# A fused chunk attention and SoLU feed-forward kernel: products with low words last in the first tiles, a new list of opening steps, six scalings and eight loads on GpSimd

## The chip, the cores and the metric

The kernel runs on one core of a Trainium2 chip. The metric is the device time of one launch in microseconds, of which the lower is the better; it is given as the median of several runs. A profiled execution is a run of its own, and its span (first to last instruction) is what the rows below are taken from.

The engines are named as the profile names them: PE (TensorE) with PEld for its weight loads, DVE (VectorE), ACT (ScalarE), POOL (GpSimd), and SP (SyncE), which here only issues DMAs. Each engine runs its instructions in the order of the program and waits where an instruction's data or buffer is not ready, so whatever stands behind a waiting instruction on its engine waits too.

## The reference

Attention inside chunks of 64 positions, and on its output (4608 tokens of 512 features) a feed-forward layer with a SoLU activation and a layer norm. Inputs are q, k and v of shape (8, 8, 576, 64) in float32; the weights w_in (512 x 1024), w_out (1024 x 512) and g_ln come in float64.

```python
scores = scale * np.matmul(q_c, k_c.transpose(0, 1, 2, 4, 3))   # chunks of 64
scores = scores - np.max(scores, axis=-1, keepdims=True)
attn = np.exp(scores)
attn = attn / (np.sum(attn, axis=-1, keepdims=True) + 1e-09)
out = np.matmul(attn, v_c)
...
h = x @ w_in
e = np.exp(h - np.max(h, axis=-1, keepdims=True))
solu = h * (e / (np.sum(e, axis=-1, keepdims=True) + 1e-09))
mu = np.mean(solu, axis=-1, keepdims=True)
var = np.mean((solu - mu) ** 2, axis=-1, keepdims=True)
ln = (solu - mu) / np.sqrt(var + 1e-06) * g_ln
return (ln @ w_out).astype(np.float32)
```

## The kernel before

**Tiles.** The 4608 tokens are 36 tiles of 128 (NT = 36). A tile passes through scores (16 small products of q and k), a softmax, values (16 small products of the attention weights and v), which give x, the first product h = x w_in (`ffn_in`, L469), the activation (`solu_a`, `solu_b`, `variance`), a transposition of z, and the second product (`ffn_out`, L587), whose result is scaled and stored.

**High and low words.** Products run on fp32r operands, so each of x, z and the weights is split in a high word and a low word (x_h and x_l, z_h and z_l, wi_h and wi_l, wo_h and wo_l), and three of the four products of words are summed: high with high, high with low, low with high. `ffn_in` is thus 24 products of 128x512 (4 chunks of the 512 features, 2 halves of the columns, 3 pairs of words), and `ffn_out` is 24 as well (8 chunks, 3 pairs). In `ffn_in` of tile 0 and in every `ffn_out`, the three pairs of a chunk come together, so a chunk's low words must be there when its high words are used.

**Weights.** The float64 weights arrive as 8 blocks of 1 MB (`load_pair`, L158, the tile w_raw), 4 of w_in and 4 of w_out. A block x is made into words by five steps: `unit_scale` (c:x, a clamp on POOL or DVE, then an activation on ACT), `unit_bits` (b:x), `unit_join` (C:x on DVE), `unit_high` (t:x on ACT) and `unit_low` (d:x on DVE). The buffers of blocks 2 to 7 are those that later hold q and k (q_st, k_st).

**The opening.** What happens before tile 5's first product is not a loop but a list of words, `START` (L18): a word names a step and a tile or block, and a word that comes a second or third time is the next part of that step. n loads q and k of one tile as they lie (nat), N transposes them on PE and copies them out of PSUM (qT, kT), v loads v, S is scores, A the maximum, the subtraction and the exponential of the softmax, B its sum, reciprocal and scaling (s_e or e), T a transposition of the attention weights on PE with four copies to attn_t, V values with x_h and x_l, M is `ffn_in`, X and Y are `solu_a` and `solu_b`, R is `variance`, z the transposition of z on PE with z_h and z_l, F a third of an `ffn_out`, o and O the scaling and the store of a tile's result, w some products of the identity matrix with no use but to keep PE at work. U and Z transpose on DVE (a_b, z_b) and, at every second tile, send 8 and 16 DMAs that finish the transposition (attn_t, z_t); half of them are issued by POOL, half by SP. Q and q load q and k of a whole batch (batch 2 here) in 32 DMAs of 32 partitions by 18 runs of 128 bytes (`qk_loads`, L253), 16 of q and 16 of k, all issued by SP; K turns them on DVE for tile 9.

`MOVED` (L34) lists the steps that run on another engine than their usual one: a copy out of PSUM on DVE in place of ACT, a clamp, `unit_bits` or the last step of `solu_b` on POOL.

**The order.** Every engine keeps the order in which the code calls it, so the list alone sets the order on each engine during the opening.

**The loop.** From tile 5 on a loop (L753) runs all tiles alike: `z_split` of the tile whose second product comes next, `ffn_in(i)`, at odd i the scores and values of the two tiles that follow, then the three thirds of an `ffn_out` of a tile three back, with the other engines' steps between. Tile 5's `ffn_in` is the loop's first work on PE; behind it stand scores of tile 8, values of tile 6, scores of 9 and values of 7, and then tile 2's `ffn_out`. `z_turn(4)` and one store are the first steps of the loop on DVE and SP.

Of the kernel before, what the change touches and what calls it, by code (L numbers as in the profile page):

```python
# [18 lines left out]
n:0 w:3 N:0:0 N:0:0 w:1 N:0:1 N:0:1 g w:1 S:0 A:0 G P:0 P:0 n:1 A:0 c:0 c:0 w:3 N:1:0 N:1:0 w:1  # L19
N:1:1 b:0 N:1:1 G P:1 w:1 S:1 B:0 v:0 C:0 A:1 t:0 T:0 T:0 c:1 c:1 w:4 V:0 V:0 P:2 b:1 c:2 n:2  # L20
d:0 P:3 A:1 n:3 w:6 N:2:0 w:1 N:2:1 C:1 V:0 B:1 t:1 c:2 T:1 N:2:0 b:2 N:2:1 T:1 d:1 S:2 n:4
M:0 M:0 C:2 t:2 c:3 c:3 v:1 A:2 A:2 b:3 d:2 C:3 N:3:0 N:3:1 N:3:1 M:0 N:3:0 S:3 N:4:0 B:2 N:4:1
t:3 N:4:0 A:3 P:5 d:3 c:5 N:4:1 A:3 T:2 T:2 S:4 V:1 M:0 P:4 n:5 B:3 T:3 V:1 V:1 M:1 X:0 X:0 T:3
A:4 A:4 b:4 v:2 N:5:1 c:4 n:6 P:7 c:5 N:5:0 c:4 Y:0 Y:0 n:7 N:5:1 V:2 b:5 v:3 B:4 N:5:0 V:2 b:7
C:4 z:0:1 P:6 v:5 N:6:0 X:1 v:4 C:5 N:6:0 S:5 Q:2 q:8 t:4 V:2 d:4 N:6:1 N:6:1 X:1 t:5 A:5 Y:1
M:2 z:0:1 z:0:1 X:2 A:5 R:0 z:0:0 z:0:0 q:8 N:7:1 q:8 c:6 S:6 Y:1 V:3 X:2 T:4 T:4 z:0:0 d:5 F
V:3 Y:2 Y:2 N:7:0 A:6 c:6 c:7 V:3 b:6 B:5 C:6 n:8 N:7:0 M:3 R:1 c:7 q:8 N:7:1 C:7 T:5 z:1:0 t:6
T:5 S:7 t:7 d:6 X:3 X:3 d:7 V:4 V:4 Y:3 Y:3 R:2 z:1:1 A:6 F F A:7 V:4 z:1:0 z:1:0 v:6 Z:2 A:7
M:4 F B:7 Z:3 o:0 V:5 z:1:1 z:1:1 B:6 F F v:7 O:0 X:4 N:8:0 X:4 U:6 U:7 V:5 Y:4 V:5 K:9 Y:4 N:8:0
R:4 R:3 N:8:1 N:8:1 o:1  # L30
# [32 lines left out]
def chunk_attention_then_solu_ffn(  # L63
# [523 lines left out]
    def ffn_out(i, part, parts):  # L587
# [8 lines left out]
        ops = []  # L596
        for fc in range(NFC):
            ops += [
                (zh[:, fc, :], wo_l[:, fc, :]),
                (zh[:, fc, :], wo_h[:, fc, :]),  # L600
                (zl[:, fc, :], wo_h[:, fc, :]),
            ]
# [251 lines left out]
```

## Time and profile before

| | us |
|---|---|
| median of 3 runs | 474.69 |
| lowest, highest | 474.67, 475.53 |
| the profiled execution, its own time | 479.38 |
| its span | 477.6 |
| its mean granted TensorE clock | 0.996 of full speed |

The profiled execution is 1.78 us longer than its span and 4.69 us longer than the median of the runs. In its page PE is busy for 98% of the span, DVE for 78%, ACT for 54%, POOL for 31%. A busy PE includes products whose ends are modelled, so the share says where PE had something in hand, and the waits are read from the time between the starts of instructions. The opening fills about the first 80 us, the loop the rest but for a tail of some 20 us.

### The profile page before, as it was taken

The numbers are of one execution on the slowest core, as the hardware profiler recorded it, in microseconds if no ns is written. First come the engines' busy times: TensorE is split into PE (matmuls) and PEld (weight loads), VectorE is DVE, ScalarE is ACT, GpSimd is POOL, SyncE is SP. The second block draws the span as 40 slices with busy tenths as digits, with TensorE's granted clock in tenths as the row PEclk, the third lists the DMA queues.
The fourth block names the chain that finished last, engine by engine and source line by source line (L and its number), as shares of the span: only waits on it lengthen the run. The fifth ranks groups of instructions, "written<-read, shape, count | busy, mean of one in ns | idle before, by whom it ended". The sixth has DMA issues, their size and how long they took to land.

```text
span 477.6 us, 11116 instructions
## 1 busy us (share of the span) xinstructions
PE 467.3 (98%) x4212; PEld 384.2 (80%) x4212; DVE 374.9 (78%) x520; ACT 256.5 (54%) x423; POOL 147.9 (31%) x298
## 2 busy tenths in 40 slices
PE   7899999899999999999999999999999999999997
PEld 5677778688888888888888888888888888888876
DVE  3999998787869887878788979797979797954441
ACT  2879884436445545454554545455555454545452
POOL 2212726050505050505050505132414142323330
PEclk9999999899999999999999999999999999999999
DMA  8999979768776878686348596848643535343221
GB/s 220 305 284 227 199 132 189 176 167 158 176 143 152 162 167 174 165 168 153 97 119 168 138 184 146 180 115 189 146 124 90 133 87 135 83 118 102 75 59 75
DMA packets 192924, 72.57 MB, mean 152 GB/s; under 512 B 177188, under 2 KB 177960, under 8 KB 191976
## 3 DMA queue, kind: packets, MB, share of 16 engines
q1 hardware_dynamic: 186056, 58.76, 55.6%
q0 software_dynamic: 6528, 12.86, 10.3%
q8 instruction: 33, 0.54, 0.5%
q10 hardware_dynamic: 288, 0.26, 0.2%
q14 instruction: 19, 0.16, 0.1%
HBM read 36.70 MB, written 9.44 MB: 97 GB/s over the span
## 4 chain that ended last, share of the span: by engine, by line
PE 86%; DVE 4%; DMA 4%; SPq 3%; ACT 2%; issue 1%; ACTq 0%; DVEq 0%
PE po L54 38%; PE ph L54 38%; PE tp L54 5%; PE sx L54 5%; SPq L54 3%; DMA nat<-in_q_dram 2%; DMA z_t<-z_b 1%; ACT attn_t L54 1%; ACT wo_h L54 1%; ACT z L54 1%; DVE z_b L54 1%; DVE h_nmax L54 0%; DMA attn_t<-a_b 0%; DVE s_sum L54 0%; DVE z L54 0%
## 5 line engine op out<-in xcount | busy, mean ns | idle before, releaser
L54 ACT ACTIVATE z<-ph,h_nmax 128x1024 f32<-128x1024 f32 x36 | 40.2, 1117 | 140.3 <-DVE h_nmax L54 140.3
L54 PE MATMUL po<-wo_l,z_h 128*128 128x512 f32 (+1 forms) x288 | 113.3, 393 | 0.1
L54 PE MATMUL ph<-wi_l,x_h 128*128 128x512 f32 x288 | 112.9, 392 | 0.0
L54 PE MATMUL ph<-wi_h,x_h 128*128 128x512 f32 x288 | 112.2, 390 | 0.0
L54 PE MATMUL po<-wo_h,z_l 128*128 128x512 f32 (+1 forms) x288 | 111.8, 388 | 0.0
L54 PE MATMUL po<-wo_h,z_h 128*128 128x512 f32 (+1 forms) x288 | 111.3, 386 | 0.0
L54 POOL DMA_DIRECT2D z_t<-z_b x144 | 71.8, 506 | 28.8 <-DVE z_b L54 24.6
L54 PE MATMUL ph<-wi_h,x_l 128*128 128x512 f32 x288 | 78.3, 390 | 0.0
L54 POOL TENSOR_TENSOR u<-ssq,eps 128x1 f32<-128x1 f32 x36 | 7.1, 198 | 214.7 <-ACT sq L54 214.4
L54 DVE TENSOR_REDUCE h_nmax<-ph 128x1 f32<-128x1024 f32 x36 | 44.0, 1222 | 31.3 <-PE ph L54 31.3
L54 PEld LDWEIGHTS po<-wo_l,z_h 128*128 128x128 f32 x288 | 54.1, 188 | 11.8 <-ACT z_h L54 0.5
L54 PEld LDWEIGHTS ph<-wi_l,x_h 128*128 128x128 f32 x288 | 54.1, 188 | 11.8 <-issue 0.4
L54 PEld LDWEIGHTS ph<-wi_h,x_l 128*128 128x128 f32 x288 | 53.9, 188 | 12.0 <-DVE x_l L54 0.7
L54 PEld LDWEIGHTS po<-wo_h,z_l 128*128 128x128 f32 x288 | 54.1, 188 | 11.7 <-DVE z_l L54 0.4
L54 PEld LDWEIGHTS ph<-wi_h,x_h 128*128 128x128 f32 x288 | 54.1, 188 | 11.0
L54 PEld LDWEIGHTS po<-wo_h,z_h 128*128 128x128 f32 x288 | 54.1, 188 | 10.5
L54 DVE TENSOR_TENSOR z_l<-z_t,z_h 128x1024 fp32r<-128x1024 f32 (+1 forms) x37 | 42.0, 1136 | 23.8 <-ACT z_h L54 22.5
L54 DVE SCALAR_TENSOR_TENSOR z<-ph,z 128x1024 f32<-128x1024 f32 x36 | 43.9, 1220 | 13.3 <-ACT z L54 13.2
L54 ACT ACTIVATE z<-z,z_sum 128x1024 f32<-128x1024 f32 x33 | 38.1, 1153 | 22.9 <-DVE z L54 22.4
L54 DVE STREAM_TRANSPOSE z_b<-z 128x1024 f32<-128x1024 f32 x34 | 41.2, 1211 | 6.2 <-ACT z L54 3.1
L54 ACT CAST z_h<-z_t 128x1024 fp32r<-128x1024 f32 (+1 forms) x37 | 35.9, 971 | 9.3 <-PE po L54 6.5
L54 ACT ACTIVATE o_sb<-po,r 128x512 f32<-128x512 f32 (+1 forms) x36 | 24.2, 673 | 27.3 <-POOL r L54 18.6
(76 smaller groups left out, 602.8 us busy)
## 6 DMA issues: line engine op xcount, KB each, us to landing
out_dram<-o_sb SPq DMA_DIRECT2D x35, 256.0 KB, 2.5
v_sb<-in_v_dram SPq DMA_DIRECT2D x32, 256.0 KB, 4.5
z_t<-z_b POOLq DMA_DIRECT2D x128, 64.0 KB, 2.7
z_t<-z_b SPq DMA_DIRECT2D x128, 64.0 KB, 2.9
q_st<-in_q_dram SPq DMA_DIRECT2D x96, 72.0 KB, 3.0
k_st<-in_k_dram SPq DMA_DIRECT2D x96, 72.0 KB, 3.2
w_raw<-in_moe_w_out_dram SPq DMA_DIRECT2D x4, 1024.0 KB, 7.9
attn_t<-a_b POOLq DMA_DIRECT2D x60, 64.0 KB, 3.8
```

The lines of the kernel that those rows point to most:

```text
L54: ins = make(*args, **kwargs)
```

## The change

It touches the opening list, four places in the code that the list calls, and one line of the loop.

- **Order of products.** `ffn_in` of tile 0 sums the pairs with wi_h for all four chunks first, in four parts (before: in parts of six with wi_l in them), and the pairs with wi_l last. `ffn_out` of tile 0 takes the pairs with wo_h first and those with wo_l last; of tiles 1 to 31 the pairs with z_h first and those with z_l in the last third; tiles 32 to 35 keep the old order. The number of products stays.
- **The list.** `START` is written anew. Block 1 of w_in is loaded whole and first, the tiles' q and k come in earlier places, and the eight first-part `ffn_out` words and both stores stand in the list (the loop's one store goes).
- **Engines.** The scaling of the softmax of tiles 0, 3, 4, 5, 6 and 7 and wi_l of block 3 move from DVE to POOL, `unit_bits` of block 0 to POOL and of block 7 to DVE, the clamp of block 1 to DVE. Of the copies out of PSUM eight run on DVE, before three. The last step of `solu_b` is on POOL for tiles 2 and 3 and on DVE for tile 4 (before: POOL for 0, 1 and 3).
- **Loads of k.** Of batch 2, the eight loads of k with heads 4 to 7 are issued by POOL.
- **Identity products.** 7 of 512 columns in place of 22 of 256.

```diff
 MOVED = """
-N:0:0=dve N:8:0=dve N:8:1=dve Y:0=pool Y:1=pool Y:3=pool b:7=pool c:0=pool c:1=pool c:2=pool
-c:3=pool c:4=pool c:5=pool c:6=pool c:7=pool
+B:0=pool B:3=pool B:4=pool B:5=pool B:6=pool B:7=pool N:0:0=dve N:0:1=dve N:1:0=dve N:1:1=dve
+N:2:0=dve N:4:0=dve N:5:0=dve N:8:0=dve Y:2=pool Y:3=pool Y:4=dve b:0=pool c:0=pool c:2=pool
+c:3=pool c:4=pool c:5=pool c:6=pool c:7=pool d:3=pool
...
-            sync.dma_start(
+            by_pool = b == 2 and src is k and h >= H // 2
+            (pool if by_pool else sync).dma_start(
...
-            sums.sort(key=lambda s: s[1])
+            sums = [(n, cc, m) for cc in range(NCC) for m in (1, 2) for n in range(2)]
+            sums += [(n, cc, 0) for cc in range(NCC) for n in range(2)]
...
-            if i == 0 and at and at % 6 == 0:
+            if i == 0 and at and at % 4 == 0:
...
+        h = NFC // 2
+        if i == 0:
+            ops = hh[:h] + lh[:h] + hh[h:] + lh[h:] + hl
+        elif i < NT - 4:
+            ops = [x for both in zip(hl, hh) for x in both] + lh
+        else:
+            ops = [x for each in zip(hl, hh, lh) for x in each]
...
-        m = ident.unsqueeze(1).to_broadcast([P, 2, P])
+        m = ident.unsqueeze(1).to_broadcast([P, 4, P])
...
             z_turn(i - 1)
-            store_one(i)
             load_batch(next_batch)
```

**SP near the end of the opening.** Before, from the loads of q of batch 2 to the attention DMAs of tiles 6 and 7 (q_st and k_st are the loads of batch 2, z_t the DMAs of tiles 2 and 3, attn_t those of tiles 6 and 7):

```order
L54 DMA q_st<-in_q_dram 32x18x32 x16
L54 DMA k_st<-in_k_dram 32x18x32 x8
L54 DMA nat<-in_q_dram 128x8x64
L54 DMA nat<-in_k_dram 128x8x64
L54 DMA k_st<-in_k_dram 32x18x32 x8
L54 DMA v_sb<-in_v_dram 128x8x64
L54 DMA z_t<-z_b 32x512 x8
L54 DMA v_sb<-in_v_dram 128x8x64
L54 DMA out_dram<-o_sb 128x512
L54 DMA attn_t<-a_b 32x512 x4
```

With the change the same stretch of SP is:

```order
L55 DMA q_st<-in_q_dram 32x18x32 x16
L55 DMA v_sb<-in_v_dram 128x8x64
L55 DMA k_st<-in_k_dram 32x18x32 x8
L55 DMA nat<-in_q_dram 128x8x64
L55 DMA nat<-in_k_dram 128x8x64
L55 DMA z_t<-z_b 32x512 x8
L55 DMA v_sb<-in_v_dram 128x8x64
L55 DMA attn_t<-a_b 32x512 x4
L55 DMA out_dram<-o_sb 128x512 x2
```

Eight loads of k and one store no longer stand ahead of the attention DMAs.

**POOL in the same part of the opening.** Before, from the small steps of `variance` of tile 1 (u and r) to the attention DMAs; the TENSOR_SCALAR on z is the last step of `solu_b` of tile 3:

```order
L54 TENSOR_TENSOR u<-ssq,eps 128x1
L54 TENSOR_TENSOR r<-u,mhalf 128x1
L54 TENSOR_SCALAR z<-z,z_sum 128x1024
L54 TENSOR_TENSOR u<-ssq,eps 128x1
L54 TENSOR_TENSOR r<-u,mhalf 128x1
L54 DMA z_t<-z_b 32x512 x8
L54 DMA attn_t<-a_b 32x512 x4
```

With the change, from the same u and r of tile 1; s_e is the scaling of tile 5, e_97 and e_98 those of tiles 6 and 7:

```order
L55 DMA k_st<-in_k_dram 32x18x32 x8
L55 TENSOR_TENSOR s_e<-e_98,s_rinv 128x512
L55 TENSOR_SCALAR z<-z,z_sum 128x1024 x2
L55 TENSOR_TENSOR e_97<-e_97,s_rinv 128x8x64
L55 DMA z_t<-z_b 32x512 x8
L55 TENSOR_TENSOR e_98<-e_98,s_rinv 128x8x64
L55 TENSOR_TENSOR u<-ssq,eps 128x1
L55 TENSOR_TENSOR r<-u,mhalf 128x1
L55 DMA attn_t<-a_b 32x512 x4
```

The eight loads now stand ahead of three scalings, two last steps of `solu_b` and both groups of DMAs.

**PE from tile 0's first product to tile 1's.** Before, each part held wi_l; these are the rows from the end of its third part on:

```order
L54 MATMUL sx<-kT,qT 64x64 x16
L54 MATMUL sx<-attn_t,v_sb 64x64 x16
L54 MATMUL ph<-wi_l,x_h 128x512
L54 MATMUL ph<-wi_h,x_h 128x512
L54 MATMUL ph<-wi_h,x_l 128x512
...
L54 MATMUL tp<-ident,s_e 128x128 x4
```

With the change, from the fourth part to tile 1:

```order
L55 MATMUL ph<-wi_h,x_h 128x512 x2
L55 MATMUL ph<-wi_h,x_l 128x512 x2
L55 MATMUL tp<-ident,nat 128x128 x4
L55 MATMUL tp<-ident,s_e 128x128 x4
L55 MATMUL ph<-wi_l,x_h 128x512 x8
L55 MATMUL tp<-ident,nat 128x128 x4
L55 MATMUL sx<-attn_t,v_sb 64x64 x16
L55 MATMUL sx<-kT,qT 64x64 x16
L55 MATMUL tp<-ident,nat 128x128 x4
L55 MATMUL tp<-ident,s_e 128x128 x4
```

All eight products with wi_l come behind the others, and a value step, a score step and three transpositions stand between them and tile 1's first product.

## Rows read from the trace of the kernel before

**Rows 1.** The page: busy us by engine, its share of the span, and instructions.

```profile
PE 467.3 (98%) x4212; PEld 384.2 (80%) x4212; DVE 374.9 (78%) x520; ACT 256.5 (54%) x423; POOL 147.9 (31%) x298
```

**Rows 2.** The chain of work that ended last, in order of time: start, us, what. From the attention DMAs to the loop's first 50 us.

```profile
86.75 2.04 DMA attn_t<-a_b
...
91.75 5.68 PE po L54 x24
97.43 5.44 PE ph L54 x24
...
115.94 5.69 PE po L54 x24
...
140.13 5.65 PE po L54 x24
```

**Rows 3.** The timeline of PE around the loop's start and one round later: start, us, instruction, count, and in brackets the idle time before it with its releaser.

```profile
85.63 0.69 PE L54 MATMUL sx<-kT,qT 64*64 64x64 f32 x32
88.20 0.45 PE L54 MATMUL sx<-attn_t,v_sb 64*64 64x64 f32 x2 [1.88 <-DMA attn_t<-a_b]
88.92 1.02 PE L54 MATMUL sx<-attn_t,v_sb 64*64 64x64 f32 x27 [0.27 <-DMA attn_t<-a_b]
...
91.68 0.50 PE L54 MATMUL po<-wo_l,z_h 128*128 128x512 f32 x1
...
113.68 0.69 PE L54 MATMUL sx<-kT,qT 64*64 64x64 f32 x32
...
115.87 0.50 PE L54 MATMUL po<-wo_l,z_h 128*128 128x512 f32 x1
```

**Rows 4.** Busy time in stretches: the stretch, its length, busy us of PE, PEld, DVE, ACT, POOL with the number of instructions, granted clock, DMA share, GB/s.

```profile
88.00:89.00 1.00, 0.52 (x6) 0.40 (x10) 1.00 (x2) 0.00 (x0) 0.00 (x0) 0.60 0.78 225
90.00:91.00 1.00, 1.00 (x49) 1.00 (x45) 0.87 (x2) 1.00 (x2) 0.00 (x0) 0.50 1.29 253
92.00:93.00 1.00, 1.00 (x6) 0.81 (x5) 0.97 (x3) 0.96 (x3) 0.00 (x0) 1.00 0.44 70
```

**Rows 5.** The timeline of SP, whose rows are DMA issues, near the end of the opening.

```profile
64.56 4.22 SPq L54 DMA_DIRECT2D k_st<-in_k_dram  x8
...
70.29 6.63 SPq L54 DMA_DIRECT2D k_st<-in_k_dram  x8
...
77.67 5.74 SPq L54 DMA_DIRECT2D z_t<-z_b  x8
...
84.89 2.44 SPq L54 DMA_DIRECT2D attn_t<-a_b  x4
```

**Rows 6.** The timeline of PE in the opening: the first product of `ffn_in` of tiles 1 and 5, and the only longer wait between tile 1 and tile 5.

```profile
34.33 0.48 PE L54 MATMUL ph<-wi_l,x_h 128*128 128x512 f32 x1
...
63.27 0.66 PE L54 MATMUL tp<-ident,z 128*128 128x128 f32 x4 [0.45 <-ACT attn_t L54]
...
80.00 0.48 PE L54 MATMUL ph<-wi_l,x_h 128*128 128x512 f32 x1
```

**Rows 7.** Busy time in stretches of 10 us of the opening, columns as in rows 4.

```profile
20.00:30.00 10.00, 9.26 (x109) 7.35 (x110) 9.86 (x14) 8.12 (x13) 1.14 (x1) 1.00 1.16 250
30.00:40.00 10.00, 9.80 (x107) 7.82 (x108) 9.86 (x14) 7.86 (x17) 2.48 (x3) 1.00 1.02 297
70.00:80.00 10.00, 10.00 (x79) 8.13 (x77) 9.74 (x16) 2.48 (x5) 5.63 (x11) 1.00 1.03 171
```

**Rows 8.** The DMA issues of the stretch 14.1 to 14.3 us, with the size of each and the us from issue to landing; the first is the fourth block of w_in.

```profile
w_raw<-in_moe_w_in_dram SPq DMA_DIRECT2D x1, 1024.0 KB, 9.9
```

**Rows 9.** The timeline of DVE: one instruction of each kind that the change moves off or onto it (wi_l is that of block 3), and the first z_b.

```profile
9.62 0.69 DVE L54 TENSOR_SCALAR w_b<-w_raw 128x1024 uint32<-128x1024 uint32 x1
...
31.02 1.22 DVE L54 TENSOR_TENSOR wi_l<-w_a,wi_h 128x1024 fp32r<-128x1024 f32 x1
...
57.68 0.68 DVE L54 TENSOR_REDUCE s_sum<-e 128x8 f32<-128x520 f32 x1
58.63 0.69 DVE L54 TENSOR_TENSOR s_e<-e,s_rinv 128x512 f32<-128x512 f32 x1
...
69.60 1.24 DVE L54 STREAM_TRANSPOSE z_b<-z 128x1024 f32<-128x1024 f32 x1
...
82.15 0.65 DVE L54 COPY qT<-tp 128x512 f32<-128x512 f32 x1
```

**Rows 10.** The timeline of POOL: two clamps, w_b, u and r of tile 1, and the eight z_t issues.

```profile
9.70 1.60 POOL L54 TENSOR_SCALAR w_a<-w_raw 128x1024 f32<-128x1024 f32 x1 [8.26 <-DMA w_raw<-in_moe_w_in_dram]
...
36.83 1.09 POOL L54 TENSOR_SCALAR w_a<-w_raw 128x1024 f32<-128x1024 f32 x1 [1.55 <-DMA w_raw<-in_moe_w_out_dram]
...
47.36 3.71 POOL L54 TENSOR_SCALAR w_b<-w_raw 128x1024 uint32<-128x1024 uint32 x1 [6.14 <-DMA w_raw<-in_moe_w_out_dram]
...
59.45 1.43 POOL L54 TENSOR_TENSOR r<-u,mhalf 128x1 f32<-128x1 f32 x1
...
73.84 4.19 POOL L54 DMA_DIRECT2D z_t<-z_b  x8 [4.54 <-DVE z_b L54]
```

**Rows 11.** Groups of POOL's instructions by form: count, busy us, mean ns of one, idle time before with its releasers.

```profile
L54 POOL DMA_DIRECT2D z_t<-z_b x144 | 71.8, 506 | 28.8 <-DVE z_b L54 24.6 <-DMA k_st<-in_k_dram 3.4 <-issue 0.7
L54 POOL DMA_DIRECT2D attn_t<-a_b x60 | 29.5, 498 | 23.0 <-PE ph L54 17.1 <-issue 5.9
```

**Rows 12.** The page's row on the queue of POOL's DMAs: packets, MB, share of the time of 16 DMA engines.

```profile
q0 software_dynamic: 6528, 12.86, 10.3%
```

More of the change, by code (lines that the diff above doesn't have):

```diff
@@ L18 @@
 START = """
[L19 to L30, printed above, removed]
+P:1 n:0 w:3 N:0:1 N:0:0 n:1 P:0 c:1 P:0 c:1 b:1 N:0:0 c:0 N:0:1 g C:1 w:1 S:0 A:0 t:1 N:1:0 n:2
@@ new lines @@
+N:1:1 N:1:0 N:1:1 A:0 B:0 w:2 S:1 n:3 N:2:0 P:2 N:2:1 v:0 d:1 N:2:0 P:3 N:2:1 A:1 T:0 T:0 S:2
+v:1 N:3:0 b:0 c:2 A:1 G c:0 N:3:0 A:2 C:0 w:1 N:3:1 B:1 c:3 n:4 A:2 N:3:1 t:0 d:0 b:2 c:2 S:3
+C:2 v:2 V:0 V:0 T:1 V:0 M:0 T:1 n:5 A:3 c:3 t:2 V:1 M:0 b:3 M:0 P:4 C:3 V:1 N:4:0 G t:3 P:5 A:3
+M:0 B:2 N:4:1 d:3 N:4:0 d:2 B:3 T:2 T:2 c:4 V:1 M:0 M:0 N:5:0 X:0 N:4:1 V:2 n:6 X:0 S:4 V:2
+N:5:0 N:5:1 Y:0 c:5 T:3 T:3 P:6 v:3 Y:0 A:4 A:4 M:1 b:4 c:6 b:5 N:5:1 B:4 c:4 c:5 C:4 z:0:0 R:0
+z:0:1 v:4 z:0:1 V:2 z:0:0 C:5 z:0:1 P:7 c:7 t:5 n:7 X:1 M:2 X:1 N:6:1 S:5 z:0:0 t:4 d:5 N:6:1
@@ L31 @@
+Y:1 Y:1 X:2 V:3 X:2 N:6:0 N:6:0 A:5 V:3 d:4 F N:7:0 N:7:0 v:6 Q:2 q:8 q:8 Y:2 S:6 V:3 b:7 c:7
+N:7:1 c:6 v:5 R:1 b:6 T:4 T:4 M:3 C:7 z:1:0 N:7:1 A:6 t:7 C:6 t:6 S:7 X:3 A:5 d:7 d:6 X:3 V:4
+A:6 V:4 q:8 q:8 z:1:1 Y:3 F F B:5 z:1:0 V:4 A:7 Y:3 Y:2 B:6 z:1:1 z:1:1 A:7 n:8 M:4 T:5 Z:2 U:6
+Z:3 X:4 F F B:7 R:3 z:1:0 v:7 X:4 F T:5 V:5 Y:4 N:8:0 K:9 V:5 Y:4 U:7 N:8:1 V:5 o:0 o:1 R:4 O:0
+N:8:1 N:8:0 O:1 R:2
 """
 MOVED = """
-N:0:0=dve N:8:0=dve N:8:1=dve Y:0=pool Y:1=pool Y:3=pool b:7=pool c:0=pool c:1=pool c:2=pool
@@ L231, in unit_low @@
         if kind == "in":
-            dve.tensor_tensor(
+            (pool if f"d:{x}" in moved else dve).tensor_tensor(
                 out=paired(wi_l[:, m, :]),
@@ L382, in softmax_b @@
         a = st[i, "e"] = work.tile([P, H, CH], F32, name="s_e") if i < PE_TURNED else e
-        dve.tensor_tensor(
+        (pool if f"B:{i}" in moved else dve).tensor_tensor(
             out=a, in0=e, in1=rinv.unsqueeze(2).to_broadcast([P, H, CH]), op=ALU.mult,
@@ L475, in ffn_in @@
         if i == 0:
-            sums.sort(key=lambda s: s[1])
+            sums = [(n, cc, m) for cc in range(NCC) for m in (1, 2) for n in range(2)]
+            sums += [(n, cc, 0) for cc in range(NCC) for n in range(2)]
         else:
             sums.sort(key=lambda s: (s[0], s[2] == 2))
+        first, last = sums[0][1:], sums[-1][1:]
         for at, (n, cc, m) in enumerate(sums):
-            if i == 0 and at and at % 6 == 0:
+            if i == 0 and at and at % 4 == 0:
                 yield
@@ L486, in ffn_in @@
                 ph[:, n, :], x[:, cc, :], w[:, cc, cols],
-                start=(cc == 0 and m == 0), stop=(cc == NCC - 1 and m == 2),
+                start=(cc, m) == first, stop=(cc, m) == last,
             )
@@ L595, in ffn_out @@
             ]
[L596 to L602, printed above, removed]
+        hh, lh, hl = (
+            [(z[:, fc, :], w[:, fc, :]) for fc in range(NFC)]
+            for z, w in ((zh, wo_h), (zl, wo_h), (zh, wo_l))
+        )
+        h = NFC // 2
[5 more added lines that the diff above has]
+            ops = [x for each in zip(hl, hh, lh) for x in each]
         n = len(ops) // parts
@@ L724, in warm @@
             pe.matmul(
-                ph[:, 0, :2 * P].rearrange("p (x m) -> p x m", x=2), ident, m, start=True, stop=True
+                ph[:, 0, :].rearrange("p (x m) -> p x m", x=4), ident, m, start=True, stop=True
             )
```

## The prediction

> **What bounds the kernel now.** I read the page first: PE is in hand for 98% of the span [rows 1], so what counts is where PE's stream starts late or breaks. The chain of waits says where. From 91.75 us on it runs on PE alone, and two tiles take 115.94 - 91.75 = 24.19 us, then 140.13 - 115.94 = 24.19 us again [rows 2]. The loop is at PE's own pace; nothing on DVE, ACT or POOL there is worth anything. What can move is the opening, up to tile 5's first product at 80.00 us [rows 6], and the joint between opening and loop.
>
> The joint is broken. After tile 5's `ffn_in` PE starts the scores of tile 8 at 85.63 and tile 2's `ffn_out` at 91.68, 6.05 us later; one round on the same steps take 115.87 - 113.68 = 2.19 us [rows 3]. The loss is 3.86 us: 1.88 + 0.27 us of waiting for attn_t, and the rest because the granted clock is 0.60, then 0.50 after that idle time (the level of 1.2 GHz) and 1.00 (2.4 GHz) again only at 92 us [rows 4]. The attention DMAs were late because SP issued them at 84.89, behind eight loads of k (6.63 us from 70.29), and the z_t issues (from 77.67) that POOL, with its own eight, had begun at 73.84 [rows 5, 10].
>
> The opening itself is nearly PE-bound from 34.33 us (tile 1's first product): 45.67 us to 80.00, with one wait of 0.45 us [rows 6]. DVE is full as well, 9.86 of 10 us from 20 to 40 us and 9.74 from 70 to 80 [rows 7].
>
> **The joint.** The change takes eight loads and a store from ahead of SP's attention DMAs. SP then reaches its z_t issues some 6.6 us earlier, at about 71 us, and is held by z_b, ready at about 73.8 [rows 5, 10]. Its eight issues take 5.7 us, so attn_t can go at about 79.5 if the data is there: tile 7's scaling is now on POOL, behind its eight z_t issues (4.19 us), so it ends at 73.8 + 4.2 and 0.6 to 1.9 us (below), about 79, and the transposition on DVE makes it 80. Issue 2.44 and landing 2.04 us after the last [rows 2, 5] give about 84.5, against 86.3 when values of tile 6 want it (85.63 plus one block of 64x64 products, 0.69 [rows 3]). So I book the whole 3.86 us: **-3.9**. What is late next is PE itself. The cover is 1.8 us; if it fails by one or two, the wait comes back with its clock loss of 1.7.
>
> **The opening, to tile 1.** Before, 34.33 us follows from block 3 of w_in, which lands at 14.16 (its issue) + 9.9 = 24.1 us [rows 8] and then needs clamp, activation, join, cast and wi_l. The new list puts q and k of tile 3 (0.5 MB) ahead of it that stood behind. The stretches from 10 to 40 us move 250 to 297 GB/s [rows 7], so it lands 1.7 to 2.0 us later, at about 26. Behind that the change shortens something: only products with wi_l wait for the last step, and these come at the end. wi_l of block 3 on POOL has no row. Its nearest are a clamp of the same size, 1.09 us, and w_b, 3.71 us, against 1.22 on DVE [rows 9, 10]; with two inputs I take the middle, 2.4, and keep both ends. In this order tile 0's last product comes at about 34, but three transpositions, a value step and a score step, some 2.6 us of PE, are then listed ahead of tile 1: its first product at 36.7, 2.4 us later. Of that, two transpositions and one value step are work that PE did after 34.33 before: 1.6 us to take off. Net **+0.8**. Bounds: -1.7 if the block lands as before and POOL is at its low end; +3 if POOL takes 3.71 us and DVE's list is late as well.
>
> The first products need wi_h of block 0, whose w_b is on POOL now: 3.71 us for 0.6. That costs nothing if the DMAs set the pace, since x_h of tile 0 waits for v of tile 0, which is behind block 2. Seven products of 512 columns for 22 of 256 cost no time where PE is idle anyway; what they may cost is in the rivals.
>
> **The opening, from tile 1 on.** PE's work is the same but for those 1.6 us, and the two third-parts of `ffn_out` stand in other places without adding any. It stays at PE's pace if DVE keeps up, and DVE's sum hardly changes: six scalings go (6 x 0.69), wi_l (1.22); five copies (5 x 0.65), a clamp and the last step of `solu_b` (0.6 to 1.2 each) come [rows 9]. ACT loses five copies. **0**, or +1 if K (1.4 us on DVE), now ahead of tile 5's x_l, is not covered by the eight products that need no x_l.
>
> **POOL.** Its new work is six scalings of 128x512 (no row; half a clamp, 0.55, to half a w_b, 1.9) and the eight loads of k. Those are the unknown. In POOL's order they stand ahead of the scaling of tile 5, two last steps of `solu_b` and all z_t and attn_t issues. POOL's DMAs take 506 ns each [rows 11], with 6528 packets in 144 + 60 DMAs, 32 each [rows 11, 12]. A load of k is 32 x 18 = 576 runs of 128 bytes. If a DMA has a fixed price, the eight are 4.0 us; if the price goes by packet, each is 18 x 0.506 = 9.1 and all are 73 us. The nearest row is the same engine's DMA, and I take 0.5 to 0.8 each.
>
> By the Trainium skill, DMA: Bandwidth & Descriptors, section Anatomy of one DMA, generating descriptors is a "small, variable" share, and many can be emitted before it shows; by that the eight would be 4.0 us too. No run here shows a DMA of POOL with more than 32 packets.
>
> How much POOL may lose: r of tile 1 ends at 60.9 us [rows 10], and is listed some 3 us earlier now; the first z_b is at 69.60 [rows 9] and needs three of the steps behind the loads, some 3.6 us. That leaves 5 to 8.5 us, 6.8 in the middle: loads of up to 0.85 us each cost **0**; above that each microsecond of POOL is one of the kernel, since z_b stands on DVE ahead of tile 4's maximum and so of everything up to tile 5.
>
> **The loop and the tail.** Tiles 1 to 31 use z_l only in the last third. A PE that never waits there gains nothing: 24.19 us per two tiles, **0**. The tail keeps its order: **0**.
>
> **The sum.** 479.38 - 3.9 + 0.8 = 476.3 for a profiled execution. That one is 4.69 us above the median of the runs, and I carry the distance over: **471.6**.
>
> **Rivals.**
>
> *POOL becomes the bound (slower).* The loads are priced by packet, in part at least. For: 18 times the packets, and the queue's mean share is all there is. Against: the fixed part is not known. It decides at (6.8 + 3.1) / 8 = 1.24 us per load. Between 0.5 and 9.1 the middle by ratio is 2.15 us: 8 x 2.15 - 6.8 - 3.1 = 7.3 us slower, 482.0. A second way to the same place is DVE: a clamp on POOL took 1.60 us from 9.70, beside DVE's w_b at 9.62, and another 1.09 [rows 9, 10]. Loads stretched so would be 0.8 us each and still covered.
>
> By the Trainium skill, SBUF: State Buffer, section SBUF: two separate sides, GpSimd can't write descriptors while DVE runs an operation that takes both ports, and a DMA of 620 ns becomes 3100 ns. By that, as an estimate, eight loads would be 24.8 us and the kernel some 15 us slower. The trace agrees in kind only: it has the 1.60 beside the 1.09, but eight z_t issues took 4.19 us, 0.52 each, beside a DVE that was busy for 9.74 of 10 us [rows 7, 10].
>
> *The stall stays (no change).* The attention DMAs get late on their new way over POOL, by 3 us beyond the estimate: half of the 3.9 us returns and with +0.8 the time is about 473.7 to 475.6. For: z_t, a scaling and four small steps now precede them on POOL. Against: 1.8 us of cover.
>
> *The opening gains too (faster by more).* Block 3 lands as before and wi_l on POOL is short: -1.7 in place of +0.8, 469.1; with tile 0's products running ahead of their low words some microseconds more, 467.5.
>
> *The clock.* Fewer identity products leave PE idle longer in the first 25 us. If it drops as it did at 88 us, each such drop costs about 1.7 us, and tile 0's products lie in it: 473.3, still faster.
>
> **How the numbers follow.** Forecast with the clock case, 469.5 to 473.7: 0.47. More gain, 467 to 469.5: 0.17. The stall stays: 0.12. POOL is the bound: 0.24, with times from 475.6 up to 482 and beyond. The range leaves out about 0.04 at the fast end and 0.15 at the slow one: 467.5 to 479.0. A measurement of this kernel can tell about 0.2% (0.95 us) from no change: faster 0.64, same 0.12, slower 0.24.
>
> **What the new profile would show.** Right: scores of tile 8 to tile 2's `ffn_out` in about 2.2 us with a granted clock of 1.00; SP's z_t issues ahead of 75 us; tile 5's first product at 79 to 82 us; 24.19 us per two tiles. Wrong: POOL's loads of k above 1.2 us each, with the scaling of tile 5 or z_b waiting for POOL; or a granted clock under 1.00 before 40 us; or tile 1's first product beyond 38 us.

## The result and the profile after

| | before | after |
|---|---|---|
| median, us | 475.53 (5 runs, 474.67 to 477.78) | 479.10 (5 runs, 478.49 to 479.91) |
| span of the profiled execution, us | 477.6 | 477.8 |
| its own time, us | 479.38 | 479.91 |

The change makes the kernel slower: after to before is 1.0078, 95% interval 1.0055 to 1.0100, that is 3.6 us. The forecast was 471.6 us in a range to 479.0. The two spans hardly differ, which is the first lesson: the profiled execution of before was 4.69 us over the median of its kernel's runs at that time, that of after 0.81 us over its own.

The page's row for PE, which answers to [rows 1]:

```profile
PE 464.0 (97%) x4184; PEld 378.8 (79%) x4184; DVE 374.4 (78%) x520; ACT 253.9 (53%) x418; POOL 158.8 (33%) x311
```

PE's timeline of after: tile 0's first products, its products with wi_l, the first product of tile 1 and of tile 5, scores of tile 8, `ffn_out` of tile 2. It answers to [rows 3, 6].

```profile
25.85 0.73 PE L55 MATMUL ph<-wi_h,x_h 128*128 128x512 f32 x2 [0.30 <-ACT x_h L55]
29.21 1.22 PE L55 MATMUL ph<-wi_h,x_l 128*128 128x512 f32 x2 [2.62 <-DVE x_l L55]
...
36.98 2.10 PE L55 MATMUL ph<-wi_l,x_h 128*128 128x512 f32 x8
...
41.47 0.48 PE L55 MATMUL ph<-wi_l,x_h 128*128 128x512 f32 x1
...
84.17 0.48 PE L55 MATMUL ph<-wi_l,x_h 128*128 128x512 f32 x1
...
89.82 0.69 PE L55 MATMUL sx<-kT,qT 64*64 64x64 f32 x32
...
92.00 0.50 PE L55 MATMUL po<-wo_l,z_h 128*128 128x512 f32 x1
```

The joint, the place where opening and loop meet, did close: 92.00 - 89.82 = 2.18 us against 6.05 [rows 3]. Yet SP's attention DMAs went out no earlier than before, at 84.79 for 84.89 [rows 5]:

```profile
84.79 2.84 SPq L55 DMA_DIRECT2D attn_t<-a_b  x4
```

What changed is PE, which came to the joint 4.19 us later itself (89.82 for 85.63) and so found the data there. Tile 1's first product is at 41.47 in place of 34.33, and tile 5's at 84.17 in place of 80.00 [rows 6]. Early in the opening PE has tile 0's x_h and then waits 2.62 us for its x_l. What that does to the clock is in the windows of after (columns as in [rows 4]):

```profile
27.00:28.00 1.00, 0.00 (x0) 0.00 (x0) 1.00 (x1) 0.73 (x2) 0.47 (x1) 0.75 0.73 159
28.00:34.00 6.00, 4.65 (x40) 3.35 (x41) 5.79 (x10) 3.82 (x5) 0.36 (x1) 0.50 1.00 252
34.00:35.00 1.00, 1.00 (x6) 0.78 (x5) 0.05 (x1) 0.09 (x1) 1.00 (x1) 0.84 0.94 352
```

While PE waits the granted clock falls to 0.50 (1.2 GHz), and tile 0's products run at it until 34 us.

Why x_l is late is in DVE's timeline of after (the joins of blocks 0 and 2 write w_a), and in POOL's beside it:

```profile
21.06 2.14 DVE L55 SCALAR_TENSOR_TENSOR w_a<-w_a,w_b 128x1024 uint32<-128x1024 uint32 x1 [0.54 <-ACT w_a L55]
...
24.69 1.22 DVE L55 TENSOR_TENSOR wi_l<-w_a,wi_h 128x1024 fp32r<-128x1024 f32 x1
25.83 0.69 DVE L55 TENSOR_SCALAR w_b<-w_raw 128x1024 uint32<-128x1024 uint32 x1
26.62 1.93 DVE L55 SCALAR_TENSOR_TENSOR w_a<-w_a,w_b 128x1024 uint32<-128x1024 uint32 x1
28.47 0.68 DVE L55 TENSOR_TENSOR x_l<-sx,x_h 128x512 fp32r<-128x512 f32 x1
```

```profile
15.27 1.84 POOL L55 TENSOR_TENSOR s_e<-e,s_rinv 128x512 f32<-128x512 f32 x1 [0.73 <-DVE s_rinv L55]
17.20 3.72 POOL L55 TENSOR_SCALAR w_b<-w_raw 128x1024 uint32<-128x1024 uint32 x1
20.99 1.13 POOL L55 TENSOR_SCALAR w_a<-w_raw 128x1024 f32<-128x1024 f32 x1
25.99 1.47 POOL L55 TENSOR_SCALAR w_a<-w_raw 128x1024 f32<-128x1024 f32 x1 [3.87 <-DVE wi_l L55]
...
63.78 5.55 POOL L55 DMA_DIRECT2D k_st<-in_k_dram  x8
...
78.39 4.00 POOL L55 DMA_DIRECT2D z_t<-z_b  x8 [2.16 <-DVE z_b L55]
```

x_h was ready at 25.8; x_l, one operation of 0.68 us, stands behind low words of block 0, the low bits and the join of block 2. Both joins lie beside a clamp on POOL and take 2.14 and 1.93 us; a join elsewhere takes 1.23. The eight loads of k took 5.55 / 8 = 0.69 us each.

x_h of tile 0 was itself late. Its cast on ACT, of after and of a second execution of before (the first of the experiments):

```profile
25.23 0.57 ACT L55 CAST x_h<-sx 128x512 fp32r<-128x512 f32 x1
```

```profile
16.59 0.59 ACT L54 CAST x_h<-sx 128x512 fp32r<-128x512 f32 x1
```

It follows the values of tile 0, which PE now takes up at 23.47 behind the scores of tile 3, and before at 14.88.

### The profile page after: what moved, and what is told of

It reads as the page before. It is cut to its first block, busy times and chain, and to the rows that moved or that the text cites. A ratio compares the mean times of both kernels' runs of the same rounds, so it can differ in the third digit from the quotient of the medians.

```text
span 477.8 us, 11069 instructions
## 1 busy us (share of the span) xinstructions
PE 464.0 (97%) x4184; PEld 378.8 (79%) x4184; DVE 374.4 (78%) x520; ACT 253.9 (53%) x418; POOL 158.8 (33%) x311
## 3 DMA queue, kind: packets, MB, share of 16 engines
q0 software_dynamic: 6912, 13.45, 11.1%
## 4 chain that ended last, share of the span: by engine, by line
PE 91%; DVE 3%; ACT 2%; DMA 1%; issue 1%; POOL 0%; SPq 0%; ACTq 0%; DVEq 0%; POOLq 0%
PE ph L55 41%; PE po L55 40%; PE tp L55 5%; PE sx L55 5%; DMA nat<-in_k_dram 1%; DVE w_a L55 1%; ACT z L55 1%; POOL s_e L55 0%; ACT attn_t L55 0%; DVE s_sum L55 0%; DVE h_nmax L55 0%; DVE wi_l L55 0%; ACT o_sb L55 0%; ACT w_a L55 0%; SPq L55 0%
## 5 line engine op out<-in xcount | busy, mean ns | idle before, releaser
L55 PE MATMUL ph<-wi_l,x_h 128*128 128x512 f32 x288 | 111.4, 391 | 0.0
L55 PE MATMUL po<-wo_h,z_l 128*128 128x512 f32 (+1 forms) x288 | 75.2, 387 | 0.0
L55 DVE TENSOR_TENSOR z_l<-z_t,z_h 128x1024 fp32r<-128x1024 f32 (+1 forms) x37 | 42.0, 1136 | 23.1 <-ACT z_h L55 21.7
L55 ACT ACTIVATE o_sb<-po,r 128x512 f32<-128x512 f32 (+1 forms) x36 | 24.2, 675 | 26.9 <-POOL r L55 20.0
```

Of the source, the lines that this page charges most:

```text
L55: ins = make(*args, **kwargs)
```

## The experiments

The kernel before was run again beside each group of runs: medians 475.23 (19 runs), 475.40 (17), 476.11 (11), 474.99 (11) and 475.24 us (16). Ratios are to these; each edited kernel has 4 to 11 runs. In the diffs a word of the list is as in the code.

### Was the joint there to be won?

**Before, once more.** No edit.

> The kernel before, unchanged, profiled once more. Theory: the stall of 3.9 us at the joint of opening and loop was peculiar to the profiled execution that the prediction read; an ordinary execution is without it, so the span is near 473 us (474.69 - 1.78), scores of tile 8 to the first product of tile 2's second matrix take about 2.2 us, and the granted clock stays 1.00 there. Rival: every execution has the stall and the profiled one is longer by 4.7 us for another reason; then the joint takes about 6.0 us again, also in a profile with a shorter span. Time against itself: ratio 1.00.

Measured 475.76 us, ratio 1.0013 (0.9999 to 1.0027). PE's timeline of this execution, span 473.5 us, at the places of [rows 3, 6]:

```profile
33.19 0.48 PE L54 MATMUL ph<-wi_l,x_h 128*128 128x512 f32 x1
...
78.62 0.48 PE L54 MATMUL ph<-wi_l,x_h 128*128 128x512 f32 x1
...
84.25 0.69 PE L54 MATMUL sx<-kT,qT 64*64 64x64 f32 x32
85.96 0.94 PE L54 MATMUL sx<-attn_t,v_sb 64*64 64x64 f32 x29 [1.02 <-DMA attn_t<-a_b]
...
87.83 0.50 PE L54 MATMUL po<-wo_l,z_h 128*128 128x512 f32 x1
```

SP's attention DMAs in it:

```profile
82.09 2.43 SPq L54 DMA_DIRECT2D attn_t<-a_b  x4
```

The wait for attn_t is 1.02 us, not 2.15, the clock stays at 1.00, and scores to `ffn_out` take 3.58 us, not 6.05. So this execution, an ordinary one by its time, has 3.58 - 2.18 = 1.4 us to give at the joint, and the rest of the 3.86 us, 2.47, was the other execution's. That one lost 1.38 us more ahead of tile 5's first product (80.00 for 78.62).

**Before, with the eight loads of k on POOL.**

```diff
-            sync.dma_start(
+            by_pool = b == 2 and src is k and h >= H // 2
+            (pool if by_pool else sync).dma_start(
```

> The kernel before with one part of the change alone: the eight loads of k of heads 4 to 7 of batch 2 issued by POOL. Theory (the stall is not in ordinary executions): no difference within 0.3%, about 475 us, the eight issues on POOL about 0.7 us each as in the changed kernel's profile, and a joint of 2.2 us. Rival (the stall is in every execution): 3.5 to 3.9 us faster than before, about 471.5 us.

Measured 475.61 us, ratio 1.0004 (0.9986 to 1.0022): no difference. Its profile has scores of tile 8 at 84.59 and `ffn_out` at 86.81, 2.22 us, so the joint closes, and POOL pays 0.69 us a load in slack:

```profile
59.80 5.53 POOL L54 DMA_DIRECT2D k_st<-in_k_dram  x8
```

```profile
79.09 2.43 SPq L54 DMA_DIRECT2D attn_t<-a_b  x4
```

Here SP's attention DMAs do go out earlier, by 3.00 us, with PE at the joint at nearly the same time (84.59 for 84.25): this run, and not the changed kernel, shows that the loads' move closes the joint. The loads are free, and the gain is smaller than the runs can tell: by the lower end of the interval 0.7 us at most, less than the 1.4 that the one profile had to give. Where the rest went is open.

### The order of the products alone

The kernel before with the new order in `ffn_in(0)` and `ffn_out`, its list as it was (`ffn_in(0)` in six parts, the last three together).

```diff
+            sums = [(n, cc, m) for cc in range(NCC) for m in (1, 2) for n in range(2)]
+            sums += [(n, cc, 0) for cc in range(NCC) for n in range(2)]
...
+        if i == 0:
+            ops = hh[:h] + lh[:h] + hh[h:] + lh[h:] + hl
+        elif i < NT - 4:
+            ops = [x for both in zip(hl, hh) for x in both] + lh
```

> The kernel before with the new order of products alone (first product of tile 0 with low words of the weights last, second products with one pair of words last), its list of steps otherwise as it was. Theory: the order of the terms is worth nothing in either direction, since PE seldom waits for a low word there; 475.2 to 475.9 us. Rival: the new order is itself a cause of the lost time, for PE then starts on products whose high words are not there; 477 us or more.

Measured 476.25 us, ratio 1.0020 (1.0011 to 1.0029). Neither expectation holds in full: the order costs some 0.9 us by itself. It is a small part of the 3.6.

### One suspect at a time, taken back from the changed kernel

**x_l of tile 0 ahead of block 0's low words and block 2's bits and join.**

```diff
-t:0 d:0 b:2 c:2 S:3 C:2 v:2 V:0 V:0 T:1 V:0 M:0
+t:0 V:0 V:0 V:0 c:2 d:0 b:2 S:3 C:2 v:2 T:1 M:0
```

> The changed kernel with the value step of tile 0 and its x_h and x_l listed ahead of the low word of block 0, w_b of block 2 and the join of block 2 (on PE ahead of the scores of tile 3). Theory: tile 0's first products wait 2.62 us for x_l because it stands behind these on DVE, and the clock then falls to half for 7 us; with x_l early the wait goes, the clock stays 1.00, and tile 1's first product comes 1.5 to 4 us earlier than 41.5 us, the kernel 1.5 to 4 us faster than the changed one, about 475 to 477.5 us. Rival (block 3 and its words set the pace, not x_l): tile 1's first product within 0.5 us of 41.5 and no difference.

Measured 480.18 us, ratio 1.0105 (1.0082 to 1.0128): not faster. The values of tile 0 now wait 1.66 us for v, the scores of tile 3 behind them 1.42 for x_l, and tile 0's products run at half clock all the same.

**The low bits of block 0 on DVE.**

```diff
-b:0=pool
```

> The changed kernel with w_b of block 0 back on DVE. Theory A (the 3.72 us of w_b on POOL stand ahead of the join of block 0 and push the clamp of block 2 beside it, where the join takes 2.14 in place of 1.22 us): the join of block 0 starts some 2 us earlier and takes 1.2 us, and the kernel is 1 to 2 us faster than the changed one, 477 to 478 us. Theory B (later waits absorb it, x_l and block 3): under 0.5 us.

Measured 480.04 us, ratio 1.0093 (1.0074 to 1.0112): not faster.

**Loads.** q and k of tile 0 ahead of block 1, v of tile 0 ahead of blocks 2 and 3.

```diff
-P:1 n:0 w:3
+n:0 P:1 w:3
...
-t:1 N:1:0 n:2
+t:1 N:1:0 v:0 n:2
...
-P:2 N:2:1 v:0 d:1
+P:2 N:2:1 d:1
```

> The changed kernel with two loads moved back: q and k of tile 0 ahead of block 1 of the weights, v of tile 0 ahead of blocks 2 and 3. Theory (late loads): the first score product, 10.7 us in the changed kernel and 7.4 before, comes back to about 8, and 2 to 3 us of it last to tile 5's first product; 476.0 to 477.2 us. Rival (the list behind it): DVE's order and PE's half clock decide, what comes earlier waits there; 478.5 to 480 us.

Measured 480.92 us, ratio 1.0122 (1.0099 to 1.0145): the rival. PE and DVE in it:

```profile
11.79 0.69 PE L55 MATMUL sx<-kT,qT 64*64 64x64 f32 x32 [3.24 <-DVE kT L55]
```

```profile
9.24 0.69 DVE L55 TENSOR_SCALAR w_a<-w_raw 128x1024 f32<-128x1024 f32 x1 [9.24 <-DMA w_raw<-in_moe_w_in_dram]
...
22.16 1.23 DVE L55 SCALAR_TENSOR_TENSOR w_a<-w_a,w_b 128x1024 uint32<-128x1024 uint32 x1 [0.54 <-ACT w_a L55]
```

k was transposed at 6.65 us, but its copy stands on DVE behind block 1's clamp, which now waits for its load until 9.24. Here the list and the order of the loads fit each other, and turning one alone made a new wait.

**The clock.** Ten more identity products of 256 columns (W) between 16 and 29 us, five of them in the wait for x_l.

```diff
-A:1 T:0 T:0 S:2
+A:1 W:1 T:0 T:0 W:1 S:2
...
-C:0 w:1 N:3:1 B:1
+C:0 w:1 W:1 N:3:1 W:1 B:1
...
-V:0 V:0 T:1 V:0 M:0
+V:0 V:0 W:1 T:1 V:0 W:5 M:0
```

> The changed kernel with ten more identity products of 256 columns between 16 and 29 us, five of them in the wait of 2.6 us for x_l of tile 0. Theory (half clock): the granted clock stays at 1.00 from 27 to 35 us, tile 0's products take 0.23 us each instead of 0.45, and 1 to 2.5 us come back; 476.5 to 478 us. Rival: what bounds tile 0 is when its x_l and the high words of blocks 2 and 3 are there, so the products only wait longer between; 478.7 to 479.5 us, clock at 1.00 all the same.

Measured 479.43 us, ratio 1.0088 (1.0075 to 1.0102): the rival again. The window shows the clock at 1.00, and PE's and DVE's timeline what stood behind it:

```profile
30.00:35.00 5.00, 4.36 (x49) 3.30 (x50) 4.79 (x9) 2.79 (x4) 0.55 (x1) 1.00 1.05 327
```

```profile
38.26 1.19 PE L55 MATMUL ph<-wi_l,x_h 128*128 128x512 f32 x4 [0.85 <-DVE wi_l L55]
```

```profile
35.36 2.85 DVE L55 TENSOR_TENSOR wi_l<-w_a,wi_h 128x1024 fp32r<-128x1024 f32 x1
```

Tile 1's first product comes at 41.87. The gain of the clock is lost in other waits: the identity products let tile 0's first product begin only at 29.20 (25.85 without them), and later ones wait for wi_l of block 2, which takes DVE 2.85 us beside POOL's wi_l of block 3 (2.68 us from 34.45).

**Loads and clock together.**

> Both edits together: two loads moved back and ten more identity products. If late loads and half clock are two separate causes, their gains add: 474.5 to 476 us, about the kernel before. If they are one and the same delay seen twice: no better than the better of the two alone, 476 to 477.5. If neither is the cause: 478.5 us or more.

Measured 479.74 us, ratio 1.0101 (1.0083 to 1.0118). By the bounds that were set neither is the cause, nor both. As each of the two edits also made a wait of its own, this is weaker than it looks: it shows that these edits bring nothing, not that late loads and half clock cost nothing.

### Engines against list

**Four copies back on ACT.**

```diff
-N:0:1=dve N:1:0=dve N:1:1=dve N:2:0=dve
```

> The changed kernel with four copies of transposed q and k (the k of tile 0, both of tile 1, the q of tile 2) moved from DVE back to ACT, which is idle for 8 of the first 17 us. Theory (DVE's list bounds tile 0): x_l of tile 0 stands behind some 2.4 us less of work, starts at 26.5 instead of 28.5, and tile 5's first product comes 1 to 2 us earlier; 477.0 to 478.2 us. Rival (the list itself): the wait for the exponential, the clamp or the joins takes its place; 478.7 to 480 us.

Measured 479.37 us, ratio 1.0074 (1.0053 to 1.0094); x_l at 28.31. The rival.

**All of the opening's steps back on their engines.**

```diff
-N:0:1=dve N:1:0=dve N:1:1=dve N:2:0=dve b:0=pool B:0=pool B:3=pool d:3=pool
+c:1=pool
```

> The changed kernel with every step of tiles 0 to 3 and of blocks 0 to 3 back on its engine of before: the four copies on ACT, the clamp of block 1 on POOL, the low bits of block 0, wi_l of block 3 and the scalings of tiles 0 and 3 on DVE. Theory (the moves between engines make the opening long, by joins and wi_l of 1.9 to 2.9 us beside work on POOL): 475.5 to 477.0 us. Rival (the new list makes it long, on whatever engines): 478.5 us or more.

Measured 479.19 us, ratio 1.0070 (1.0048 to 1.0092). The new list is as slow on the old engines. With the list this run keeps the new order of products, the fewer identity products, the loads on POOL and the moves of the later tiles and blocks.

**The same moves put on the kernel before**, with its own list.

> The kernel before, its list as it was, with the moves between engines of the opening alone: those that the run above takes back, put on. Theory (the moves): 477 to 479 us. Rival (the list): within 0.2% of the kernel before, 475 to 476.3 us.

Measured 479.45 us, ratio 1.0084 (1.0065 to 1.0103). The moves alone are as slow on the old list:

```profile
17.11 0.70 PE L55 MATMUL tp<-ident,s_e 128*128 128x128 f32 x4 [2.73 <-POOL s_e L55]
```

There the low bits of block 0 on POOL (3.76 us from 11.13) and the scaling behind them (2.08 from 14.97) hold up the first transposition of attention weights.

So each half costs some 3 to 4 us by itself (3.3 and 4.0 by the ratios), and both together no more. What they have in common is that block 3's join ends late on DVE. DVE's busy time from the start to the end of that join, in windows (columns as in [rows 4]) of the kernel before (its second execution), of the changed kernel, of the changed kernel on the old engines, and of the kernel before with the moves:

```profile
0.00:27.06 27.06, 24.34 (x229) 18.46 (x230) 19.60 (x27) 17.41 (x27) 6.08 (x14) 1.00 1.04 267
```

```profile
0.00:32.41 32.41, 22.34 (x254) 12.77 (x255) 22.41 (x31) 16.11 (x24) 10.14 (x15) 0.92 1.04 255
```

```profile
0.00:31.97 31.97, 22.33 (x254) 13.20 (x255) 19.92 (x28) 17.95 (x28) 6.84 (x14) 0.92 1.07 259
```

```profile
0.00:32.89 32.89, 26.55 (x229) 20.32 (x230) 21.40 (x30) 15.46 (x23) 10.96 (x15) 0.95 0.89 246
```

Block 3's join ends 5.35 us later in the changed kernel: DVE worked 2.8 us longer and waited 2.5 us more (10.0 for 7.5). Of the 2.8 us, 1.6 are the two joins beside clamps on POOL (2.14 and 1.93 us for 1.22). On the old engines the work is nearly as before (19.92 for 19.60), but DVE waits 12.05 us: for an exponential behind two copies on ACT, for a cast behind a copy that PE's identity product held up. With the moves on the old list it works 1.8 us longer and waits 4.0 us more.

**Engines back, loads of tile 0 first with their copies ahead of block 1's steps, eight more identity products.**

```diff
-P:1 n:0 w:3 N:0:1 N:0:0 n:1 P:0 c:1 P:0 c:1 b:1 N:0:0 c:0 N:0:1 g
+n:0 P:1 w:3 N:0:1 N:0:0 n:1 P:0 c:1 P:0 N:0:0 N:0:1 c:1 b:1 c:0 g
```

> The changed kernel with the engines of the opening back, q and k of tile 0 loaded first and their copies ahead of block 1's steps, v of tile 0 ahead of block 2, and eight more identity products of 256 columns. Theory (several gates of like length in a row, of which each hides the others): now all are gone and the time is that of the kernel before, 474.5 to 476.5 us. Rival: what is left of the new list still costs 2 us or more; 477.5 us or more.

Measured 480.82 us, ratio 1.0114 (1.0093 to 1.0136). The rival: PE now waits 1.61 us for q of tile 1, whose load stands behind block 1, and then 1.67 for the copy of its k, which stands on ACT behind block 1's cast.

### Where along the list

**The lists joined crosswise at tile 1's first product.** In each the words of the first list up to M:1, with their engines, then what is left of the other list in its order. The third is the first with tile 0's products in the order of before.

> The list of before up to tile 1's first product, with its engines and identity products, and the changed list from there on, with the rest of the change. Theory (all that is lost is lost ahead of tile 1): tile 1's first product at 34 to 35.5 us, the end of the opening no later than before, no wait at the joint; 473.5 to 475.5 us. Rival (the new list only pays later for what its first part did ahead, and the loss comes up behind tile 1): 476.5 us or more.

> The reverse: the changed list and engines up to tile 1's first product, the list of before from there on. Theory (all that is lost is lost ahead of tile 1): tile 1's first product at about 41 us, 478.5 to 480.5 us. Rival (the part behind tile 1 has its share): 476 to 478 us.

> As the first of these three, but with tile 0's first product in the order of before, low words among the others. Theory (that order alone cost the 0.2% of the run with the order of products alone): 0.5 to 1 us faster than the first of the three, 472.8 to 475 us. Rival (it was the order of the second products): the same time as the first of the three within 0.4 us.

Measured 479.97 (ratio 1.0101, 1.0084 to 1.0117), 482.65 (1.0158, 1.0141 to 1.0175) and 478.64 us (1.0074, 1.0060 to 1.0088). The first has tile 1 at 35.15, as its theory wants, and then this:

```profile
45.27 2.25 PE L54 MATMUL tp<-ident,z 128*128 128x128 f32 x8 [2.50 <-ACT z L54]
```

PE waits at the seam, and the clock is at 0.50 from 45 to 50 us. It may be that the later part of the new list counts on softmax and activation steps that its own first part has got through; this was not tried. The runs thus tell nothing clean of where the loss lies, and the theory that they were made for stays unproved. Only the third against the first is a plain comparison: tile 0's product order is worth 1.3 us there, somewhat more than the 0.5 to 1 that was expected.

**DVE's waits cleared by hand**, on the old engines, then the same with identity products. Both loads of q and k ahead of the weights, the exponential ahead of block 1's cast, x_l ahead of block 0's low words.

```diff
-P:1 n:0 w:3 N:0:1 N:0:0 n:1 P:0 c:1 P:0 c:1 b:1 N:0:0 c:0 N:0:1 g C:1 w:1 S:0 A:0 t:1
+n:0 w:3 N:0:1 N:0:0 n:1 P:1 N:0:0 N:0:1 P:0 P:0 c:1 c:1 g w:1 S:0 A:0 A:0 b:1 C:1 t:1
...
-N:3:1 t:0 d:0 b:2 c:2 S:3 C:2 v:2 V:0 V:0 T:1 V:0 M:0
+N:3:1 S:3 v:2 V:0 V:0 V:0 d:0 b:2 c:2 c:3 C:2 T:1 M:0
```

> The changed kernel with the engines of the opening back and the waits that DVE then had in the first 25 us taken out of the list: q and k of tiles 0 and 1 loaded ahead of the weights, the first exponential ahead of block 1's cast, no identity product ahead of tile 3's k, v of tile 0 loaded earlier, x_l of tile 0 ahead of block 0's low words and block 2's join. Theory (what is lost is DVE's time ahead of block 3's high words, be it by work or by waits): x_l of tile 0 at 24 to 26 us in place of 28.5, tile 1's first product at 38 to 39.5 in place of 41.5, 476 to 478 us. Rival (the loss is not there): 478.7 us or more.

> The same with ten more identity products of 256 columns where PE idles between 14 and 26 us. Theory: with DVE's waits gone the clock is what is left; it stays at 1.00 and another 1 to 1.5 us come back, 475 to 476.5 us. Rival: as with these products alone, they bring nothing; the time of the run above within 0.5 us.

Measured 487.24 (ratio 1.0246, 1.0215 to 1.0276) and 487.33 us (1.0254, 1.0231 to 1.0277): much slower. PE's row for the scores of tile 1:

```profile
18.63 1.13 PE L54 MATMUL sx<-kT,qT 64*64 64x64 f32 x32 [6.85 <-ACT kT L54]
```

Block 1 lands later, and its activation and cast stand on ACT ahead of tile 1's copies: one wait cleared made a longer one.

**DVE's list made shorter.** The joins of blocks 0 to 3 left out of the changed kernel.

```diff
+        if x < 4:
+            bits.pop(x)
+            return
```

> The changed kernel without the join of the low bits in blocks 0 to 3 (four operations of DVE, 6.5 us in its trace; the weights of the first product then lack their lowest bits). Theory (DVE's list bounds the opening): 3 to 6 us come back, 473.5 to 476.5 us. Rival (DVE only seems to bound it, and loads, ACT or PE's half clock stand right behind): at most 1.5 us, 477.5 us or more.

Measured 477.08 us, ratio 1.0034 (1.0019 to 1.0048) against 1.0078 (1.0055 to 1.0100) with them: about 2 us of the 3.6 come back for 6.5 us of DVE, between theory and rival. In its profile x_l of tile 0 is at 26.50 in place of 28.47, and tile 5's first product at 81.09 in place of 84.17:

```profile
81.09 0.47 PE L55 MATMUL ph<-wi_l,x_h 128*128 128x512 f32 x1
```

This is the only edit of the changed kernel that gave a good part back, and it is the one that takes work from DVE without moving a step. It does two things at once, though: it shortens DVE's list, and it takes a step out of every block's own way from the load to its high word, since the cast no longer waits for the join. Which of the two gave the 2 us is not separated. And it leaves out more than the lowest bits: the join also shifts the scaled word by three bits, so the run is one of time alone.

## Why the prediction was wrong

**The loop, the POOL loads, block 3: right.** Two tiles still take 24.2 us. The loads of k cost 0.69 us each, inside the 0.5 to 0.8 booked at 0, so the rival by packets fell, and so did the estimate of 15 us by the Trainium skill, SBUF: State Buffer, section SBUF: two separate sides. No run tells which of DVE's operations beside the loads take both ports. Block 3 landed at 25.7 ("about 26"), wi_l on POOL took 2.71 us (2.4).

**"So I book the whole 3.86 us: -3.9": size wrong, and the way not taken.** The ordinary execution of before holds 1.4 us there. In the changed kernel z_t went out at 78.12, not "ahead of 75 us", and SP's attn_t at 84.79, not at the 80 of the working: what they wait for was late with the rest of the opening. The joint closed all the same, because PE was late too, so the sign "scores of tile 8 to tile 2's `ffn_out` in about 2.2 us" came true for another reason than the one given. That is luck; the mechanism itself is shown by the run with the loads alone. One run of the changed kernel (the low bits on DVE) waited 0.50 us for attn_t.

**"I carry the distance over": the first step that failed.** The profiled execution was 4.69 us over the median, and by the second execution 2.47 us of that was the very stall that the sum had just taken off (6.05 for 3.58). It was counted twice, once as a gain and once as distance. With 1.4 for 3.9 and the median as the base the same working gives 474.69 - 1.4 + 0.8 = 474.1: no change.

**"Net +0.8" for the opening: the second, and the one that gave the wrong sign.** Tile 5's first product moved by +4.17 against the profile of before, +5.55 against the second execution. With +5.55 in the corrected sum the time is 474.69 - 1.4 + 5.55 = 478.8, and 479.10 was measured. In the prediction's terms: "tile 0's last product comes at about 34" came out at 39.08 (36.98 + 2.10), while the 2.6 us from there to tile 1 were right (2.39). Two of its own signs of being wrong came, "tile 1's first product beyond 38 us" and "a granted clock under 1.00 before 40 us".

The split, against the second execution: tile 1's first product at 41.47 for 33.19, 8.28 us later; from there to tile 5 42.70 for 45.43 us, 2.7 us shorter, where 1.6 was foretold. The first part can be read in the windows up to tile 1's first product (before's second execution, then after):

```profile
0.00:33.19 33.19, 30.17 (x349) 22.91 (x349) 25.55 (x36) 22.28 (x36) 6.66 (x15) 1.00 1.04 285
```

```profile
0.00:41.47 41.47, 31.40 (x361) 20.22 (x361) 29.14 (x40) 20.93 (x33) 15.82 (x19) 0.92 1.01 262
```

PE idles 10.07 us of its stretch for 3.02, +7.05, and is busy for 1.23 us more; the two make up the 8.28. The idle time is thus nearly all of it. Some groups of PE in the same windows, before's second execution and after:

```profile
L54 PE MATMUL ph<-ident 128*128 128x256 f32 x42 | 12.2, 425 | 1.4 <-POOL ident masks.py:199 1.4
...
L54 PE MATMUL ph<-wi_h,x_h 128*128 128x512 f32 x8 | 3.2, 394 | 0.0
L54 PE MATMUL ph<-wi_h,x_l 128*128 128x512 f32 x8 | 3.1, 392 | 0.0
```

```profile
L55 PE MATMUL ph<-ident 128*128 128x512 f32 x14 | 9.5, 812 | 1.4 <-POOL ident masks.py:199 1.4
...
L55 PE MATMUL ph<-wi_h,x_h 128*128 128x512 f32 x8 | 3.7, 550 | 0.3 <-ACT x_h L55 0.3
L55 PE MATMUL ph<-wi_h,x_l 128*128 128x512 f32 x8 | 3.5, 533 | 2.6 <-DVE x_l L55 2.6
```

The identity products are 2.7 us less, so part of the idle time stands where they stood, and the products of tile 0 with wi_h are 0.9 us more (times of a group overlap those of others, so the groups don't add up to the 1.23). Of the idle time 2.6 us are the wait for x_l; the rest is in many waits of 0.2 to 1.3 us, for copies, scalings and loads. None of it was in the prediction. It looked at one chain, block 3 and its words, and asked DVE only whether its sum changes over the whole opening ("DVE's sum hardly changes"). Ahead of block 3's join DVE does change, by 2.8 us of work and 2.5 of waiting, and PE waits for x_l there. "That costs nothing if the DMAs set the pace, since x_h of tile 0 waits for v of tile 0" did not hold in this trace: v had landed by 21.7 (issued at 15.27, 6.4 us on the way), and x_h waited for PE's order, x_l for DVE's list. v stood close behind, though: in two of the edited runs (x_l early, the low bits on DVE) the values of tile 0 waited 1.66 and 0.50 us for it.

**The clock rival.** The clock did drop, for longer than it did at 88 us before. PE is busy for 4.65 of the 6 us at 0.50, so by an estimate from that row at most half of it, 2.3 us, is the clock's. But with the clock held at 1.00 the time stayed the same, in a run that put other waits in its place. The clock alone does not give the loss back; that it is only a sign of the idle time is argued.

**What is shown and what is open.** Shown: the stall at the joint was in large part that of one execution, and without it there was no gain that the runs can tell; the loads are free; the order of products costs 0.9 us alone; the opening's moves between engines cost 3 to 4 us alone, and so does the change without them; leaving out the four joins gives about 2 us back, and ten more identity products, with the clock at 1.00, give nothing. Argued from the traces only: that DVE's list ahead of block 3's join carries the whole of it. Open: how the loss is spread over the list's single steps, since no order made by hand was better, and whether the joins cost as work on DVE or as a step on each block's way. No kernel here beat the one before.
